# Four weight tiles of the first chunk fetched later, input transposes and score steps moved by some slots, three input tiles on another queue

## The chip, the cores and the metric

The kernel runs on one core of a Trainium2 chip. A core has five engines with an instruction stream each: TensorE (PE in the profile, with its weight loads shown apart as PEld), VectorE (DVE), ScalarE (ACT), GpSimd (POOL) and SyncE (SP). DMA transfers are issued from an engine's stream, here from SP and from ACT, and run beside the engines. The metric is the time of one execution on the device in microseconds (us). Three runs of the kernel before took 578.94, 583.47 and 583.84 us; their median is 583.47 us.

## What is computed

The input x has 2048 rows of 576 numbers in bfloat16. One layer norm feeds two branches, and the result is x plus both:

```python
xn = layernorm(x)                      # per row, no scale or shift
# A: sliding-window attention, 32 heads of 18, each query sees itself and the 255 keys before it
q, k, v = split(xn @ wqkv)             # 576 x 1728
o = softmax(mask(q @ k.T * 18**-0.5)) @ v
a = o @ wo                             # 576 x 576
# B: gated feed-forward layer
h = silu(xn @ w1) * (xn @ w3)          # 576 x 4608, twice
b = h @ w2                             # 4608 x 576
out = x + a + b
```

## The kernel before

**Chunks and phases.** The 2048 rows are worked off in four chunks (c = 0 to 3) of 512 rows, that is four tiles of 128 rows. Each chunk has two phases. The first runs 36 *units* (u = 0 to 35, loop at L824). A unit makes 128 of the 4608 hidden columns: nine *slots* (n = 0 to 8, L829), each a pair of matmuls (`unit_pairs`, L621), 18 matmuls in all. Then ScalarE takes a tanh (L629) and VectorE two multiplications (L635, L638) that leave the hidden columns in `hT`. The second phase multiplies `hT` with w2 (L671) and the attention's output with wo (L677), in two halves of 288 output columns, adds x and stores the result (L684, L686). Into the second phase are woven the projections of the next chunk (L399, L413).

**Attention between the units.** Into the slots of the first phase the loop puts *score steps* (`score_step`: four to six matmuls at L516, one exponential on ScalarE at L525, one or two mask multiplications on GpSimd at L552), 32 of them in chunk 0 and 40 in each later chunk. A step writes the two PSUM banks `SC`. When a quarter of the steps is done and 20 slots have gone by, a PV group follows (L573, 72 small matmuls); there are three in the first phase. Its result is scaled, transposed on VectorE and packed into `oT` by four or five small DMAs on SP's queue (`o_pack`, L606), over the next four units (`later`).

**The next chunk's input.** For each of the next chunk's four row tiles the loop places three things by tables of units (L785, L786): layer-norm statistics (`stat`), its application (`apply`), and the transpose `xn_turn` (`xt`: ten small transposes on PE at L370 into the same two banks `SC`, then one VectorE copy at L377 into `xnT`). In chunk 0 the four transposes stand in units 5, 9, 19 and 26.

**The planner.** A counter `clock` counts slots. `nxt` is the slot from which the next score step is due, and `soon` the earliest slot for it; after a transpose both are pushed on by `XT_AFTER` = 6 slots (L833), since the step overwrites the banks that the copy at L377 still reads. In chunk 0 the first step is due at slot 17 (L791). Nothing here is timed on the chip: the counter sets the order of the instructions, and the engines wait on each other by semaphores.

**Weights.** w3 and w1 come in fills of 512 hidden columns, so one fill serves four units. A fill (`load_w13`) is two halves of 576 KB: the w3 half is issued on SP's queue, the w1 half, from unit 3 on, on ACT's. Three buffers (`NW13` = 3) are used in turn. After unit 3, 7, 11, and so on to 31, the loop issues the fill that reuses the buffer just finished (L845, L846). In the text *fill f* is the one that units 4f to 4f+3 of chunk 0 read: fills 0, 1 and 2 are issued before the loop, fill 3 after unit 3, fill 6 after unit 15, fill 8 after unit 23. Fills issued after unit 27 and 31 are for the next chunk. w2 comes in tiles of 288 KB (`load_w2`, L327, always on SP's queue), four buffers in turn; 18 tiles serve a second phase. In chunk 0 the first four tiles are issued after units 8, 10, 12 and 14 (L881); every later one when the tile that it replaces has been used (L675).

**Queues.** SP issues, in the order of the program, the first weights, the fills' halves, `w2`, the x tiles, the small `repack` moves of q and k in the first units (L470), `o_pack` and the stores. A DMA issue takes its place in SP's stream, so one that has to wait holds up all behind it. ACT's queue carries the w1 halves, part of the `repack` moves and, at the start, two of the four x tiles.

```python
        for t in range(TB):
            xslot[t] = load_x(t, ("sp", "act")[t % 2])
...
                    if u in xt and n == 7:
                        xn_turn((c + 1) * TB + xt[u], SC)()
...
                if c == 0 and u in (8, 10, 12, 14):
                    load_w2()
```

Of the kernel before, what the change touches and what calls it, by code (L numbers as in the profile page):

```python
# [164 lines left out]
def bass_parallel_sum__sliding_block__glu_gated_swiglu__prompt_kernel(  # L165
# [32 lines left out]
    with ExitStack() as es:  # L198
# [93 lines left out]
        def load_x(t, eng="sp"):  # L292
            nonlocal xp_ctr
            s = xp_ctr % NXP
            xp_ctr += 1
            add(eng, lambda e: e.dma_start(xp[s][:], x2[t * 128:(t + 1) * 128, :]), w=[("xp", s)], dma=f"xp{s}")
            return s
# [391 lines left out]

        xslot = {}  # L690
        for t in range(TB):
            xslot[t] = load_x(t, ("sp", "act")[t % 2])
        add("sp", lambda e: e.dma_start(
            wa[:, 0:4, 2 * D:3 * D], A_wqkv[0:512, 2 * D:3 * D].rearrange("(kd p) f -> p kd f", p=128)),
            w=["wv"], dma="wv")
# [81 lines left out]
        aside = [m for g in held[3:] for m in repack_moves(0, g, "act")]  # L777
        aside_at = {u: 1 for u in (2, 3, 5, 6, 8, 9, 11, 14, 15, 17, 18, 21, 22, 24)}

        PV_COST, XT_COST, XT_AFTER, PV_AFTER = 6.6, 0.8, 6, 20  # L780

        for c in range(NC):
            NS = len(steps_of(c))
            att = [(g, s) for g in range(G) for s in range(NS)]
            near = {0: (2, 3, 5), 1: (6, 7, 9)} if c == 0 else {0: (0, 2, 4), 1: (4, 6, 8)}  # L785
            near.update({2: (15, 17, 19), 3: (23, 24, 26) if c == 0 else (24, 26, 28)})  # L786
            plan = near if c + 1 < NC else {}
            stat, apply, xt = ({v[k]: i for i, v in plan.items()} for k in range(3))
            loads = {0: () if c == 0 else (1,), 8: (2,), 17: (3,)} if c + 1 < NC else {}
            total = 9 * NF + len(att) + 3 * PV_COST + len(xt) * XT_COST  # L790
            start = 17 if c == 0 else 5  # L791
            last = total - 12
            nxt = soon = start
            clock = 0.0
            done = 0
            pv_ready = {}
            free = [("pt", n) for n in range(NPT)]
            if c:
                free += [("sh", n) for n in range(4)]
            early = [("h", n) for n in range(4)]  # L800
            side = {}
            jobs = {}
            next_pv = 0

            def later(u, what):
                side.setdefault(u, []).append(what)

            def take(n):
                if n < len(early) and c == 0:
                    return early[n]  # L810
                return free.pop(0)

            def score_step():
                nonlocal done
                g, s = att[done]
                scores(c, g, s)
                sl = take(done)
                exps(c, g, s, sl)
                masks(c, g, s)
                done += 1  # L820
                if done % (2 * NS) == 0:
                    pv_ready[done // (2 * NS) - 1] = clock + PV_AFTER

            for u in range(NF):  # L824
                if u in loads:
                    for i in loads[u]:
                        xslot[(c + 1) * TB + i] = load_x((c + 1) * TB + i)
                b0 = jobs[u] = job()
                for n in range(9):  # L829
                    if u in xt and n == 7:  # L830
                        xn_turn((c + 1) * TB + xt[u], SC)()
                        clock += XT_COST
                        nxt = soon = max(nxt, clock + XT_AFTER)  # L833
                    into = nxt - (clock + 9 - n)
                    if done < len(att) and (clock >= nxt or (n == 8 and into < 3 and clock >= soon)):
                        if not (u in xt and n < 7 and n > 1):
                            score_step()
                            soon = clock + 7.5
                            room = last - clock - PV_COST * (3 - next_pv) - 5 * sum(v > u for v in xt)
                            nxt = max(soon, clock + room / max(1, len(att) - done))  # L840
                            clock += 1
                    unit_pairs(c, u, n, n + 1, b0[0])
                    clock += 1
                unit_tanh(u, b0[0])
                if u % 4 == 3 and u < NF - 4:  # L845
                    load_w13((), "act")  # L846
                if next_pv in pv_ready and clock >= pv_ready[next_pv] and next_pv < 3:
                    j = next_pv
                    next_pv += 1
                    banks = job()  # L850
                    pv(c, j, banks)
                    clock += PV_COST
                    for g in (2 * j, 2 * j + 1):
                        for s in range(NS):
                            if pt_of[(c, g, s)][0] != "h":
                                free.append(pt_of[(c, g, s)])
                    later(u, lambda b=banks: (pv_out(b[0], 0), pv_out(b[1], 1), o_scale(0)))
                    later(u + 1, lambda j=j: (o_turn(2 * j, 0), o_turn(2 * j, 1), o_scale(1)))
                    later(u + 2, lambda j=j: (o_turn(2 * j + 1, 0), o_pack(2 * j, "sp")))
                    later(u + 3, lambda j=j: o_turn(2 * j + 1, 1))  # L860
                    later(u + 4, lambda j=j: o_pack(2 * j + 1, "sp"))
                unit_h(u, b0[0])
                for what in side.pop(u, []):
                    what()
                if u in stat:
                    t = (c + 1) * TB + stat[u]
                    for part in range(2):
                        ln_stats(t, xslot[t], part)
                if u in apply:
                    t = (c + 1) * TB + apply[u]  # L870
                    ln_apply(t, xslot[t])
                if c == 0 and u in (1, 6, 9):
                    repack(0, held.pop(0), "sp")
                if c == 0:
                    for _ in range(min(aside_at.get(u, 0), len(aside))):
                        aside.pop(0)()
                if c == 0 and u == 25:
                    add("sp", lambda e: e.dma_start(
                        wo[:, 0:4, :], A_wo[0:512, :].rearrange("(kd p) f -> p kd f", p=128)), w=["wo"], dma="wo")
                    add("sp", lambda e: e.dma_start(wo[0:64, 4, :], A_wo[512:576, :]), j=["wo"], dma="wo")  # L880
                if c == 0 and u in (8, 10, 12, 14):  # L881
                    load_w2()
                if u == 29:
                    xs = [load_x(c * TB + tt) for tt in range(TB)]
            assert done == len(att) and next_pv == 3 and not aside, (done, next_pv, len(aside))
            ring_of[:] = [*jobs[NF - 2], *jobs[NF - 1]]
            ring_ctr = 0
            ACC[:] = [*job(), *SC]
            proj = iter([])
            if c + 1 < NC:  # L890
                for g in range(G):
                    keep_keys(g)
                proj = (None for gen in (qk_atoms(c + 1, lambda c, g: repack(c, g, "act", ("act", "sp")[g % 2])), v_atoms(c + 1)) for _ in gen)
                xn_swap(c + 1, ("sp", "act"))
            proj_at = [36 + 8 * i for i in range(9)] + [116 + 24 * i for i in range(2 * TB)]
            banks = ()
            for n, item in enumerate(p2_list(c)):
                p2_item(c, item, xs)
                if n in (36, 70):
                    load_w13_half()  # L900
                if n == 3:
                    for u in sorted(side):
                        for what in side.pop(u):
                            what()
                elif n == 19:
                    banks = (ring(), ring())
                    pv(c, 3, banks)
                    pv_out(banks[0], 0)
                    pv_out(banks[1], 1)
                    o_scale(0)  # L910
                    o_turn(6, 0)
                    o_turn(6, 1)
                    o_pack(6, "act")
                    o_scale(1)
                    o_turn(7, 0)
                    o_turn(7, 1)
                    o_pack(7, "act")
                elif n == 100 and c + 2 < NC:
                    xslot[(c + 2) * TB] = load_x((c + 2) * TB)
                elif n in proj_at:  # L920
                    next(proj, None)
            for _ in proj:
                pass
# [31 lines left out]
```

## Time and profile before

| What | Value |
|---|---|
| median of three runs | 583.47 us (578.94, 583.47, 583.84) |
| the profiled execution: its own time | 584.11 us |
| its span, first to last instruction | 582.2 us |
| mean granted TensorE clock | 0.997 |
| PE busy | 567.8 us (98%) |
| DVE, ACT, POOL busy | 338.8 us (58%), 239.0 us (41%), 161.8 us (28%) |
| bytes by DMA | 83.60 MB, mean 144 GB/s |
| chunk 0: unit 0 starts, second phase starts | 24.48 us, 113.25 us |

The profile is taken by the hardware on one execution; its instruction times are exact to some ten nanoseconds, matmul ends are modelled. Busy shares are means over the whole span, and the stages have different limits: the start is set by loads, the first phase of each chunk by PE, and in chunk 0 by the DMAs beside it. Line numbers such as L621 are those of the kernel. `ps<-xnT,w` means that the PSUM tile `ps` is written from `xnT` and a tile whose name begins with `w`; buffer numbers are left out, so w13 and w2 buffers both appear as `w` and are told apart by line (L310 and L327) and size. The time of a DMA from issue to landing includes what it waits behind others in its queue.

### The profile page before, as it was taken

How to read it: one execution, taken by the hardware profiler on the slowest of the kernel's cores; microseconds unless marked ns; L12 is line 12 of the kernel's file. 1: busy time of each engine (PE TensorE's matmuls, PEld its weight loads, DVE VectorE, ACT ScalarE, POOL GpSimd, SP SyncE). 2: the span in 40 equal slices, each digit the busy share in tenths (PEclk: the TensorE clock that was granted, in tenths of full speed). 3: DMA queues.
4: the chain of work that ended last, by engine and by line, in shares of the span. 5: the costliest groups of instructions: out<-in, count | busy, mean ns of one | idle time of the engine just before them, and what ended most of it. 6: DMA issues, size and time to landing. Idle time of an engine off the chain costs nothing.

```text
span 582.2 us, 15317 instructions
## 1 busy us (share of the span) xinstructions
PE 567.8 (98%) x6548; PEld 337.9 (58%) x6558; DVE 338.8 (58%) x636; ACT 239.0 (41%) x310; POOL 161.8 (28%) x377
## 2 busy tenths in 40 slices
PE   8999979999999999999999999999999999999998
PEld 4445434567765555556776555446677554544776
DVE  7577956742348687764325868775331567667311
ACT  4166645400027677640003666862000577666000
POOL 6233433400004344540002343544000234433000
PEclk9999989999999999999999999999999999999999
DMA  8989998869644857776963567687676276541452
GB/s 227 189 151 183 168 195 181 168 135 197 163 118 85 171 105 140 158 149 143 196 149 95 127 133 156 119 165 163 137 169 150 74 143 124 136 91 52 122 154 62
DMA packets 118963, 83.60 MB, mean 144 GB/s; under 512 B 25520, under 2 KB 117808, under 8 KB 118896
## 3 DMA queue, kind: packets, MB, share of 16 engines
q1 hardware_dynamic: 82325, 60.31, 48.0%
q10 hardware_dynamic: 36571, 22.32, 20.0%
q8 instruction: 51, 0.84, 0.7%
q14 instruction: 16, 0.13, 0.1%
HBM read 71.07 MB, written 2.36 MB: 126 GB/s over the span
## 4 chain that ended last, share of the span: by engine, by line
PE 87%; DMA 5%; ACT 2%; DVE 2%; SPq 2%; issue 1%; ACTq 0%
PE ps L621 42%; PE ps L671 24%; PE ps L516 5%; PE ps L399 5%; PE ps L677 3%; PE ps L573 3%; DMA w<-in_B_w_dram 3%; PE ps L413 3%; DMA kv<-stage 1%; DMA wa<-in_A_wqkv_dram 1%; ACT pt L525 1%; SPq L470 1%; ACT th L629 1%; DVE hT L638 1%; DVE gs L635 1%
## 5 line engine op out<-in xcount | busy, mean ns | idle before, releaser
L525 ACT ACTIVATE pt<-ps 128x1024 bf16<-128x1024 f32 (+1 forms) x118 | 119.3, 1011 | 234.5 <-PE ps L516 233.0
L621 PE MATMUL ps<-xnT,w 64*128 64x512 bf16 x1440 | 190.6, 378 | 4.6 <-DMA w<-in_B_w_dram 4.5
L621 PE MATMUL ps<-xnS,w 64*128 64x512 bf16 x1152 | 156.3, 377 | 0.1
L671 PE MATMUL ps<-w,hT 128*128 128x288 bf16 x1152 | 154.8, 286 | 0.0
L552 POOL TENSOR_TENSOR pt<-pt,mk 128x128 int32<-128x128 int32 (+1 forms) x211 | 85.5, 428 | 237.2 <-ACT pt L525 236.8
L635 DVE SCALAR_TENSOR_TENSOR gs<-th,ps 128x512 bf16<-128x512 bf16 x144 | 98.1, 681 | 82.0 <-ACT th L629 81.2
L671 PEld LDWEIGHTS ps<-w,hT 128*128 128x128 bf16 x1152 | 112.0, 98 | 35.6 <-issue 1.7
L621 PEld LDWEIGHTS ps<-xnT,w 64*128 64x128 bf16 x1440 | 68.7, 94 | 66.3 <-DMA w<-in_B_w_dram 5.0
L638 DVE SCALAR_TENSOR_TENSOR hT<-gs,ps 128x512 bf16<-128x512 bf16 x144 | 98.9, 687 | 4.9
L629 ACT ACTIVATE th<-ps 128x512 bf16<-128x512 f32 x144 | 85.6, 594 | 38.4 <-PE ps L621 36.0
L621 PEld LDWEIGHTS ps<-xnS,w 64*128 64x128 bf16 x1152 | 57.4, 94 | 54.5 <-issue 1.5
L516 PE MATMUL ps<-qv,kv 64*128 64x320 bf16 (+2 forms) x720 | 58.5, 252 | 1.1 <-DMA kv<-stage 0.6
L516 PEld LDWEIGHTS ps<-qv,kv 64*128 64x128 bf16 x720 | 34.6, 94 | 38.8 <-issue 2.7
L684 DVE TENSOR_TENSOR ofin<-ps,xp 128x288 bf16<-128x288 f32 x32 | 14.7, 458 | 68.0 <-PE ps L677 68.0
L403 DVE CAST stage<-ps 128x512 bf16<-128x512 f32 x36 | 24.8, 689 | 36.0 <-PE ps L399 35.7
L428 DVE CAST va<-ps 64x288 bf16<-64x288 f32 x56 | 25.5, 455 | 28.8 <-PE ps L413 28.2
L399 PE MATMUL ps<-xnT,wa 128*128 128x512 bf16 x153 | 37.1, 379 | 0.4
L525 ACT ACTIVATE stage<-ps 128x1024 bf16<-128x1024 f32 x30 | 30.7, 1023 | 13.9 <-PE ps L516 13.7
L595 DVE STREAM_TRANSPOSE od<-oq 128x256 bf16<-128x256 bf16 x64 | 25.8, 427 | 6.3 <-POOL oq L588 6.3
L552 POOL TENSOR_TENSOR stage<-stage,mk 128x128 int32<-128x128 int32 (+1 forms) x54 | 21.9, 427 | 17.3 <-ACT stage L525 17.3
L588 POOL TENSOR_TENSOR oq<-uq,rden 128x288 bf16<-128x288 f32 x16 | 10.8, 674 | 53.1 <-DVE rden L587 53.1
L677 PE MATMUL ps<-wo,oT 128*128 128x288 bf16 x160 | 25.3, 286 | 0.0
(56 smaller groups left out, 271.5 us busy)
## 6 DMA issues: line engine op xcount, KB each, us to landing
w<-in_B_w_dram SPq DMA_DIRECT2D x42, 576.0 KB, 7.1
w<-in_B_w_dram SPq DMA_DIRECT2D x72, 288.0 KB, 3.4
w<-in_B_w_dram ACTq DMA_DIRECT2D x30, 576.0 KB, 8.3
xp<-in_A_x_dram SPq DMA_DIRECT2D x30, 144.0 KB, 5.9
out_dram<-ofin SPq DMA_DIRECT2D x32, 72.0 KB, 2.1
kv<-stage ACTq DMA_DIRECT2D x91, 18.0 KB
oT<-od SPq DMA_DIRECT2D x84, 18.0 KB
xnS<-xnT SPq DMA_DIRECT2D x5, 256.0 KB, 4.4
```

The lines of the kernel that those rows point to most:

```text
L399: add("pe", lambda e, kd=kd, ws=ws: e.matmul(PS[:, b, :], ws, xnT[:, c % 2, kd, :], start=(kd == 0), stop=(kd == 4)), r=["w8" if i == 8 el ...
L428: add("dve", lambda e, dst=dst, src=src: e.tensor_copy(dst, src), r=[("ps", b), ("ps", b + 1)], **kw)
L516: add("pe", lambda e, r0=r0, out_=out_, kb=kb, q0=q0, nb=nb: e.matmul(out_, kv[r0:r0 + 64, g, kb + NV - NB, :], qv[r0:r0 + 64, g, q0 * KB: ...
L525: add("act", lambda e: e.activation(pt_slot(sl)[:, 0:w, :], PS[:, SC[0]:SC[1] + 1, 0:w].rearrange("p r q -> p q r"), ACT.Exp, scale=scale) ...
L552: add("pool", lambda e, vb=vb, mm=mm: e.tensor_tensor(vb, vb, mm, ALU.mult), r=(key if n == 0 else []) + ["mk"], **{"w" if n == 0 else "j" ...
L595: add("dve", lambda e: e.transpose(od[i][:, c0:c0 + CH // 2], oq[:, c0:c0 + CH // 2]), r=["oq", "oq0"], **{"j" if half else "w": [("od", i)]})
L621: add("pe", lambda e, n=n, r0=r0, r=r, k=k, src=src: e.matmul(PS[:, b0 + r, :], w13[sl][r0:r0 + 64, k, fl * 128:(fl + 1) * 128], src, star ...
L629: add("act", lambda e: e.activation(th[i][:], PS[:, bg, :], ACT.Tanh, scale=0.5), r=[("ps", bg)], w=[("th", i)])
L635: add("dve", lambda e: e.scalar_tensor_tensor(out=gs[i][:], in0=th[i][:], scalar=1.0, in1=PS[:, bg, :], op0=ALU.add, op1=ALU.mult), r=[("t ...
L638: add("dve", lambda e: e.scalar_tensor_tensor(out=hT[:, u, :], in0=gs[i][:], scalar=0.5, in1=PS[:, bu, :], op0=ALU.mult, op1=ALU.mult), r= ...
L671: add("pe", lambda e: e.matmul(bank, hT[:, f, tt * 128:(tt + 1) * 128], w2[sl][:, k, :], start=(f == 0), stop=False), r=[("h", f), ("w2", ...
L677: add("pe", lambda e: e.matmul(bank, oT[:, k, tt * 128:(tt + 1) * 128], wo[:, k, d0:d0 + HD], start=False, stop=(k == 4)), r=[("oT", g) fo ...
```

## The change

It has four parts:

- In chunk 0 the first four w2 tiles are issued after units 20, 22, 24 and 26 rather than 8, 10, 12 and 14.
- The input transposes `xn_turn` stand before slot 8 of their unit rather than slot 7, in all chunks that have them. No score step is put into slots 2 to 8 of such a unit (before: 2 to 6).
- After a transpose the next score step is due 8 slots later in chunk 0 and 5 slots later in the other chunks (before: 6 in all). The first step of chunk 0 is due at slot 20 (before: 17).
- Of the first four x tiles, tile 0 is loaded by SP's queue and tiles 1, 2 and 3 by ACT's (before: 0 and 2 by SP's, 1 and 3 by ACT's).

```diff
         xslot = {}
         for t in range(TB):
-            xslot[t] = load_x(t, ("sp", "act")[t % 2])
+            xslot[t] = load_x(t, "act" if t else "sp")
...
-        PV_COST, XT_COST, XT_AFTER, PV_AFTER = 6.6, 0.8, 6, 20
+        PV_COST, XT_COST, PV_AFTER = 6.6, 0.8, 20
...
-            start = 17 if c == 0 else 5
+            start = 20 if c == 0 else 5
...
                 for n in range(9):
-                    if u in xt and n == 7:
+                    if u in xt and n == 8:
                         xn_turn((c + 1) * TB + xt[u], SC)()
                         clock += XT_COST
-                        nxt = soon = max(nxt, clock + XT_AFTER)
+                        nxt = soon = max(nxt, clock + (8 if c == 0 else 5))
                     into = nxt - (clock + 9 - n)
                     if done < len(att) and (clock >= nxt or (n == 8 and into < 3 and clock >= soon)):
-                        if not (u in xt and n < 7 and n > 1):
+                        if not (u in xt and n > 1):
                             score_step()
...
-                if c == 0 and u in (8, 10, 12, 14):
+                if c == 0 and u in (20, 22, 24, 26):
                     load_w2()
```

## The prediction

> **What bounds the kernel.** First the busy times and the slices of the page.
>
> ```profile
> PE 567.8 (98%) x6548; PEld 337.9 (58%) x6558; DVE 338.8 (58%) x636; ACT 239.0 (41%) x310; POOL 161.8 (28%) x377
> ...
> DMA  8989998869644857776963567687676276541452
> ```
>
> PE is busy for all but 14.4 of 582.2 us. The change removes no matmul, so nearly all that it can win is PE's idle time. The DMA row shows where loads could matter: its first six slices (14.55 us each, up to 87 us) read 8 or 9. So next, PE's waits:
>
> ```profile
> PE ps L621 <- DMA w<-in_B_w_dram: 4.5, 2, 4.1
> ...
> PE ps L370 <- ACT pt L525: 1.1, 5, 0.3
> ...
> PE ps L516 <- DMA kv<-stage: 0.6, 1, 0.6
> PE ps L413 <- DMA wa<-in_A_wqkv_dram: 0.6, 1, 0.6
> PE ps L516 <- DVE xnT L377: 0.5, 2, 0.2
> ```
>
> Each is a wait that one part of the change touches. The largest is for a fill. PE's timeline puts both in chunk 0: 0.39 us at 71.89 (unit 20, fill 5) and 4.12 us at 84.78 (unit 24, fill 6). The chain that ended last, around the second:
>
> ```profile
> 65.39 1.62 PE ps L621 x15
> 67.01 17.72 DMA w<-in_B_w_dram
> 84.73 0.05 issue
> 84.78 3.25 PE ps L621 x12
> ```
>
> Fill 6's w3 half was issued at 67.01 and landed 17.72 us later. SP's timeline shows what it stood behind:
>
> ```profile
> 57.83 0.48 SPq L327 DMA_DIRECT2D w<-in_B_w_dram  x1
> 58.36 0.93 SPq L310 DMA_DIRECT2D w<-in_B_w_dram  x1
> 59.33 3.31 SPq L327 DMA_DIRECT2D w<-in_B_w_dram  x1
> 62.69 3.77 SPq L606 DMA_DIRECT2D oT<-od  x4
> 66.49 0.47 SPq L327 DMA_DIRECT2D w<-in_B_w_dram  x1
> 67.01 0.70 SPq L310 DMA_DIRECT2D w<-in_B_w_dram  x1
> ```
>
> L327 are w2 tiles, not read before 113.25; L310 are the w3 halves of fills 5 and 6. ACT's half of fill 6 went out at 61.38, when unit 15 had freed the buffer: SP was 5.6 us later. The stages (columns: busy us of the five engine rows, then granted clock, DMA share, GB/s):
>
> ```profile
> 84.78:88.03 3.25, 3.25 (x20) 1.23 (x22) 1.03 (x3) 0.00 (x0) 0.38 (x2) 0.57 1.15 201
> ...
> 25.00:85.00 60.00, 54.52 (x706) 27.36 (x704) 44.06 (x83) 34.16 (x46) 20.45 (x49) 0.99 1.05 170
> 92.00:108.00 16.00, 15.76 (x236) 7.84 (x236) 12.56 (x23) 9.95 (x14) 5.63 (x13) 1.00 0.66 145
> ```
>
> From 25 to 85 us the DMAs are saturated at 170 GB/s, from 92 to 108 a third is free. After the long wait the clock was 0.57.
>
> **The w2 tiles.** Nothing is added or dropped: four issues of 0.4 to 3.3 us on SP and 4 x 288 KB = 1.18 MB move by some 25 us. At 170 GB/s the bytes are 6.9 us of DMA time, 1.73 a tile. Does every fill then come in time? I take each landing of before, less the tiles no longer ahead of it, against the new start of its unit.
> - Fill 5: landed 71.85 (58.36 + 13.5), two tiles fewer: 68.4. Unit 20 could have started at 71.50. Earlier waits that go (below: 0.3 + 0.5 + 0.24) bring it to 70.46; the second PV group (69.78 to 71.11, 1.33) and two steps of 0.2 now follow unit 20's start, so 68.7. A dead heat: 0.3 of slack. I keep 0.1 us of its 0.39.
> - Fill 6: landed 84.73, four tiles fewer: 77.8. Unit 24: 84.78 - 4.12 - 0.39 - 1.04 - one step 0.2 = 79.0. Slack 1.2. The 4.12 us go.
> - Fill 7: ACT's half landed at 83.8 (69.90 + 13.9), SP's between the x tile before it (73.44 + 12.9 = 86.4) and fill 8, by bytes near 90.7; less 6.9: 83.8. Unit 28: units 24 to 27 took 11.63 (84.78 to 96.41); without the slow clock's 1.31 (below), a wait of 0.24, a PV group (1.0) and one step it is 8.9, so 87.9. Slack 4.
> - Fill 8: landed 95.74 (81.47 + 14.3), less 6.9, plus the two tiles now ahead of it, 3.5: 92.3. Unit 32: units 28 to 31 took 8.6 (to 105.0), with the PV group and a step more 9.8, so 97.7. Slack 5.4.
>
> What is late next is thus fill 5, then fill 6, by about a microsecond. On SP the tiles are moved past `o_pack`; fill 6's half now stands ahead of the first `o_pack`, which is a unit later with its PV group, so it can go at 61.4. The last w2 tile goes out after unit 26, near 86; even with the longest landing seen, 17.7, it is there at 103.7, before the second phase (113.25 less the 7.0 us that chunk 0 saves in all: 106.2).
>
> The clock: at 84.78 18 matmuls took 3.25 us; the same 18 take 1.94 elsewhere. So 1.31 us more go with the wait, 5.43 in all. After the 0.39 us wait the matmuls kept their 1.03 to 1.04 us for eight.
>
> The Trainium skill, "TensorE: Matmul & The Clock Gate" (Part 1: The HAM clock gate), says that the clock falls to half after an idle window of about 3.4 us and stays so for a window; by it the loss would be an estimated 1.7 us and the sum 0.4 higher, and a remainder under 3.4 us might cost no clock. The trace agrees in kind, with 1.31.
>
> **First steps of chunk 0.** The first step waited 0.60 us at 28.93 for the small `repack` moves, which landed at 28.88. Three slots later (3 x 1.94 / 9 = 0.65) PE passes 28.93 with other matmuls; as PE itself comes earlier, I take 0.5 (bounds 0 and 0.6). The same 32 steps are issued; each delays its exponential (0.9 to 1.0 us, ACT 41% busy) and masks (0.43 each, POOL 28%) equally.
>
> **Transposes.** In chunk 0 the step after a transpose waited 0.24 us twice for the copy at L377; it stands two to three slots (0.43 to 0.65) later: 0.48 gone. VectorE's copy comes at most one slot later. In chunks 1 and 2 the transposes waited for the exponential of the step before, which reads the same banks: 1.1 us in five waits (0.15 to 0.26). One more pair of matmuls ahead of each covers 0.216: I take 1.0 (at most 1.1). The next step stays where it was, five pairs behind rather than six. In chunk 1 the first copy ended at 180.90 and the step began at 181.49; it would begin at 181.27, still after the copy. If that cover of 0.37 is gone, six steps wait some tenths and the term turns to about -1, its lower bound.
>
> **x tiles.** SP loses one issue of 0.42 us ahead of the projection weights, for which PE waited 0.58 at 8.91; ACT gets one more ahead of a 1.28 us table load that ends at 3.0, its first real work coming at 6.89. Bounds: nothing, as the last weights took 6.7 us to land and the bytes are the same, and 0.43. Nearest row: the issue. I take 0.3.
>
> The Trainium skill, "DMA: Bandwidth & Descriptors" (Issuing engines are not separate DMA queues), says that DMAs of several engines share the same DMA engines, and that spreading saves issue time only. By that, with the bytes unchanged, this term might be 0 and the sum 0.3 lower; no run here shows it yet.
>
> **Sum.** 5.43 + (0.39 - 0.1) + 0.5 + 0.48 + 1.0 + 0.3 = 8.0 us; at most 8.4. The profiled execution took 584.11 us (span 582.2 and 1.9 around it), 0.64 above the median. 584.11 - 8.0 = **576.1 us**.
>
> **Rivals.**
> - *The wait comes back in part* at unit 20 or 24. For: both slacks are near one microsecond, an estimate from a mean rate; one run of before was 5 us faster, so landings vary. Against: fills 5 and 6 lose exactly the bytes that stood ahead. A wait of 2 to 5 us: 578 to 581.
> - *It doesn't do what it says*: the small moves, not the w2 tiles, hold fill 6 up, and the 5.43 stay. For: 128-byte pieces ride in the same queues. Against: two w2 tiles landed 13.8 and 16.8 us after issue, within the same stretch. Only the other terms, 2.6: 581.5.
> - *Slower: the second phase starves.* The tiles' 6.9 us of DMA time meet 5.4 free us between 92 and 108 (a third of 16), in a first phase 7.0 shorter: a backlog of up to 8.5 us where the second phase starts. Its fifth tile is asked for when the first is used up and took 5.5 us (issue at 115.42). Four tiles of 16 matmuls last 7.9 us; from there on a longer fetch stops PE. 5.5 + 8.5 is 6 too long; with the clock (1.3) and as much again on the next tiles, 9: 585. Against: a PV group and the projections lie between, and L671 has no DMA wait now.
>
> **Chances.** Forecast (574.5 to 578) 0.64, returning wait 0.20, no effect 0.09, starving 0.07. One per cent, about what a measurement can tell from no change, is 5.8 us, so the bounds are 577.6 and 589.3: most of the first case lies below 577.6 (0.56); its rest (0.08), the next two (0.29) and a mild starving (0.03) lie within; starving through many tiles lies above 589.3 (0.04). The range is the first two cases, 574.5 to 581.
>
> **What would show it.** Right: no PE wait over 0.5 us between 25 and 113, fill 6's SP half issued near 61.4 and landed before 79, the second phase starting near 106, no dip of the clock, no wait of L370 on L525. Wrong: a fill's wait at units 20 to 32; a DMA wait at L671 soon after the second phase starts; new waits of L516 on L377 in chunks 1 and 2.

## The result and the profile after

The changed kernel takes **576.09 us** (median of 8 runs, 574.94 to 577.53) and the kernel before 582.84 us (median of 8, 578.94 to 584.25): a ratio of 0.9898, 95% interval 0.9867 to 0.9928. It is faster by 1.0%. The forecast was 576.1. A second series gave 574.88 (6 runs) against 583.15, ratio 0.9864, interval 0.9833 to 0.9895.

The profiled execution took 574.94 us, 1.1 less than the median, with a span of 573.1 us; that of before took 584.11, 1.3 more than its median. So the two profiles stand 9.2 us apart, and the medians 6.7. This matters below.

The page, parts 1 and 2, and then PE's waits of the whole span, all of them:

```profile
PE 565.3 (99%) x6548; PEld 337.8 (59%) x6558; DVE 338.6 (59%) x636; ACT 238.5 (42%) x310; POOL 161.4 (28%) x377
...
DMA  8989999998627585877762658696666367441552
```

```profile
PE ps L702 <- DVE oq L697: 1.2, 1, 1.2
PE ps L573 <- issue: 1.0, 2, 0.7
PE ps L357 <- DVE xn L347: 0.9, 2, 0.7
PE ps L621 <- DMA w<-in_B_w_dram: 0.5, 1, 0.5
PE ps L413 <- DVE va L428: 0.3, 1, 0.3
```

All five waits that the prediction listed are gone. L370 on L525, L516 on the small moves and L516 on L377 are not in the list any more; at L413 a wait of 0.3 us for VectorE stands where 0.58 for the weights stood; the one wait for a fill that is left, 0.45 us, is a new one (fill 3, at unit 12). The chain that ended last runs on PE up to unit 24's start (78.55) and passes there to ScalarE, where before it ran 17.72 us through a DMA:

```profile
76.33 1.94 PE ps L621 x18
78.27 0.24 PE ps L516 x4
78.51 0.02 issue
78.53 0.02 ACT pt L525
```

SP's timeline for the same stretch. L310 "x2" holds the halves of fills 5 and 6 (56.24 and 60.3), L606 are the first `o_pack` moves, the L310 at 69.61 belongs to fill 7, L327 is the first w2 tile:

```profile
56.24 4.73 SPq L310 DMA_DIRECT2D w<-in_B_w_dram  x2
61.51 3.15 SPq L606 DMA_DIRECT2D oT<-od  x4
...
69.61 0.83 SPq L310 DMA_DIRECT2D w<-in_B_w_dram  x1
70.48 0.63 SPq L327 DMA_DIRECT2D w<-in_B_w_dram  x1
```

And two of the stages shown of before (busy us of PE, PEld, DVE, ACT, POOL; clock, DMA share, GB/s):

```profile
92.00:108.00 16.00, 16.00 (x225) 8.94 (x202) 12.51 (x22) 9.25 (x14) 8.82 (x22) 1.00 1.13 208
25.00:85.00 60.00, 59.34 (x766) 28.95 (x764) 47.19 (x90) 35.73 (x49) 21.52 (x52) 1.00 0.95 169
```

PE is idle for 0.66 of 60 us in the first phase of chunk 0, where it was 5.48. The DMAs have lost their slack between 92 and 108 us: two of the moved w2 tiles land in it (at 93.91 and 101.79), and with chunk 0 shorter the fills of the next chunk come earlier too.

### The profile page after: what moved, and what is told of

Read it like the earlier page. It is cut to its first block, busy times and chain, and to the rows that moved or that the text cites. A ratio compares the mean times of both kernels' runs of the same rounds, so it can differ in the third digit from the quotient of the medians.

```text
span 573.1 us, 15316 instructions
## 1 busy us (share of the span) xinstructions
PE 565.3 (99%) x6548; PEld 337.8 (59%) x6558; DVE 338.6 (59%) x636; ACT 238.5 (42%) x310; POOL 161.4 (28%) x377
## 4 chain that ended last, share of the span: by engine, by line
PE 91%; DMA 3%; DVE 3%; SPq 1%; issue 1%; ACTq 0%; POOL 0%; ACT 0%
PE ps L621 45%; PE ps L671 24%; PE ps L399 6%; PE ps L516 6%; PE ps L573 4%; PE ps L677 3%; PE ps L413 3%; DMA w<-in_B_w_dram 3%; SPq L470 1%; DVE xn L347 1%; DMA xp<-in_A_x_dram 0%; DVE va L428 0%; PE ps L370 0%; DVE hT L638 0%; DVE gs L635 0%
## 5 line engine op out<-in xcount | busy, mean ns | idle before, releaser
L525 ACT ACTIVATE pt<-ps 128x1024 bf16<-128x1024 f32 (+1 forms) x118 | 119.3, 1011 | 228.5 <-PE ps L516 227.0
L671 PE MATMUL ps<-w,hT 128*128 128x288 bf16 x1152 | 154.8, 286 | 0.1
L671 PEld LDWEIGHTS ps<-w,hT 128*128 128x128 bf16 x1152 | 112.0, 98 | 35.7 <-issue 1.9
L516 PE MATMUL ps<-qv,kv 64*128 64x320 bf16 (+2 forms) x720 | 58.5, 252 | 0.2
L516 PEld LDWEIGHTS ps<-qv,kv 64*128 64x128 bf16 x720 | 34.8, 94 | 37.2 <-ACT stage L525 1.5
L525 ACT ACTIVATE stage<-ps 128x1024 bf16<-128x1024 f32 x30 | 30.7, 1023 | 13.7 <-PE ps L516 13.5
```

The lines of the kernel that those rows point to most:

```text
L516: add("pe", lambda e, r0=r0, out_=out_, kb=kb, q0=q0, nb=nb: e.matmul(out_, kv[r0:r0 + 64, g, kb + NV - NB, :], qv[r0:r0 + 64, g, q0 * KB: ...
L525: add("act", lambda e: e.activation(pt_slot(sl)[:, 0:w, :], PS[:, SC[0]:SC[1] + 1, 0:w].rearrange("p r q -> p q r"), ACT.Exp, scale=scale) ...
L671: add("pe", lambda e: e.matmul(bank, hT[:, f, tt * 128:(tt + 1) * 128], w2[sl][:, k, :], start=(f == 0), stop=False), r=[("h", f), ("w2", ...
```

## The experiments

Fill landings are the time of issue plus the time to landing of the later half. In each table row, "before" is the kernel before in the same series.

| Kernel | Median us | before | Ratio, 95% interval | Executions with clock 0.999 or 1.000 |
|---|---|---|---|---|
| w2 tiles moved, nothing else (`w2_only`) | 578.18 | 582.13 | 0.9942 (0.9915 to 0.9969) | 10 of 10 |
| third and fourth tile moved (`w2_two`) | 577.61 | 582.13 | 0.9913 (0.9881 to 0.9945) | 9 of 10 |
| tiles at the old units, by ACT's queue (`w2_by_act`) | 581.80 | 582.13 | 0.9990 (0.9960 to 1.0019) | 3 of 10 |
| changed kernel, tiles moved back (`undo_w2`) | 578.71 | 582.13 | 0.9949 (0.9922 to 0.9976) | 9 of 10 |
| slots alone (`slots_only`, 4 runs) | 577.12 | 583.25 | 0.9898 (0.9838 to 0.9958) | 4 of 4 |
| slots alone again (`slots_again`) | 577.41 | 583.15 | 0.9907 (0.9874 to 0.9939) | 6 of 6 |
| changed kernel again (`after_again`) | 574.88 | 583.15 | 0.9864 (0.9833 to 0.9895) | 6 of 6 |
| x tiles alone (`x_only`) | 583.58 | 583.25 | 1.0020 (0.9985 to 1.0055) | 2 of 10 |
| matmuls into the wait (`keep_busy`) | 583.21 | 583.25 | 0.9999 (0.9962 to 1.0036) | 7 of 10 |
| first `o_pack` later (`opack_later`) | 583.49 | 583.15 | 1.0007 (0.9972 to 1.0042) | 5 of 10 |
| tiles later still (`w2_late`, 4 runs) | 576.05 | 583.15 | 0.9892 (0.9847 to 0.9937) | 4 of 4 |

A second profile of the unchanged kernel (`before_again`) took 585.78 us.

The last column counts the executions in which the mean granted clock of TensorE shows no dip. It speaks for executions that were not profiled: the profiled one of before has 0.997 with one dip, `before_again` 0.994 with one twice as long. Of the 67 executions of before in these series 26 had 0.999 or 1.000 (median 579.9 us), 29 had 0.997 (583.3 us) and 12 had 0.994 to 0.996 (586.3 us).

### The w2 tiles alone

```diff
-                if c == 0 and u in (8, 10, 12, 14):
+                if c == 0 and u in (20, 22, 24, 26):
```

> The kernel before with one edit: the first four w2 tiles are issued after units 20, 22, 24 and 26. Theory (their bytes hold up fills 5 and 6): fill 5 lands near 68.4 and fill 6 near 77.8 us, ahead of units 20 (70.9) and 24 (80.3); the waits of 0.39 and 4.12 us and the slow clock's 1.31 go, 5.8 us in all: 578.3 for an execution like the profiled one of before (584.11), ratio about 0.990. Rival (the slots and the x tiles carry the gain, the w2 tiles little): the wait of 3 to 4 us at unit 24 stays, within 1 us of before.

Its profiled execution took 578.22 us, 5.89 less than the one of before: the 5.8 forecast for it. Fill 5 was there at 66.4 (56.4 + 10.0), fill 6 at 73.3 (63.2 + 10.1); units 20 and 24 began at 70.97 and 79.57. PE's waits in this kernel between 25 and 113 us:

```profile
PE ps L516 <- DMA qv<-stage: 0.7, 1, 0.7
PE ps L516 <- DVE xnT L377: 0.6, 3, 0.2
```

No fill among them. The rival falls: the tiles alone remove both waits, and the clock was full in all ten executions. But the median fell by 3.95 only, since the median execution of before (582.13) is 2.0 faster than the profiled one.

### Two tiles moved

```diff
+                if c == 0 and u in (8, 10, 20, 22):
```

> The kernel before with only the third and fourth w2 tiles moved, to after units 20 and 22; the first two stay after units 8 and 10. Theory (1.73 us of DMA time a tile): fill 5 lands as before (wait of 0.4 at unit 20), fill 6 lands 3.5 us earlier, near 81.2: a wait of 0.6 at unit 24, and no dip of the clock. About 4.8 us faster than before in an execution like the profiled one, 579.3. Rival (the four issues on SP, not the bytes): fill 6's half leaves near 62 to 63 us and the wait goes wholly.

Two tiles are enough: units 20 and 24 began at 71.47 and 80.07 with no wait (unit 12 waited 0.71 us for fill 3), and the time is that of moving all four within the intervals. The 1.73 us a tile would have left 0.6 us, so the price per tile was too low. Fill 6's half left at 65.0, not at 62 to 63.

### The tiles on ACT's queue

```diff
-            add("sp", lambda e: e.dma_start(
+            add(eng, lambda e: e.dma_start(          # eng = "act" for the first four tiles
                 w2[s][:], ...
```

> The kernel before, but the four w2 tiles go out at the same units 8, 10, 12 and 14 on ACT's queue rather than SP's. Same bytes at the same time; SP's stream is free of their issues, so fill 6's half can go 3 to 5 us earlier. Theory (bytes): fill 6 is whole near 84 us all the same, now with ACT's half the late one; a wait of 3 to 5 us in all at units 20 and 24 stays, 582 to 585 us. Rival (late issue on SP, or the order in SP's queue, is what makes fill 6 late): the wait goes, about 578.

No difference in the median, as the theory had it; but not in its way. In the profiled execution (581.41) fill 6's SP half left at 65.45 and landed 15.1 us later, at 80.6, and unit 24 began at 82.57 without a wait. The time had been lost ahead of it: unit 0 began at 25.40 rather than 24.48, which the edit cannot have done, as the first moved tile goes out at 46.77; units 12 and 20 waited 0.66 and 0.26 us. But this execution had the full clock, and seven of the ten had 0.997, the figure of the profiled before: in most of them a dip remained, as the theory would have it, though no profile shows where. Which of the two theories is right this run does not tell.

### The changed kernel with the tiles moved back

> The changed kernel with the w2 tiles back after units 8, 10, 12 and 14. Theory: fills 5 and 6 land as in before, 71.9 and 84.7; units 20 and 24 come earlier than in before (68.6 and 78.6), so PE waits some 3 us at unit 20 and 2 to 3 at unit 24, 5 to 6 us in all; each is shorter than the 4.12 of before, so the clock may stay full. 581 to 583 us, about 5.5 above the changed kernel. Rival (the gain is in the other parts): 577.

Between the two: taking the tiles back costs 2.6 us against the changed kernel's 576.09, half of what was expected. PE's waits from 25 us to the second phase:

```profile
PE ps L573 <- issue: 1.8, 1, 1.8
PE ps L621 <- DMA w<-in_B_w_dram: 1.1, 2, 0.8
PE ps L621 <- issue: 0.2, 1, 0.2
```

The fills cost 1.1 us, at units 12 and 20, not 5 to 6. (The stall of 1.8 us in the PV group, of which the last section tells, comes ahead of unit 24, which began at 81.86; without it fill 6 would have been some 0.8 us late there.) Fill 6's SP half left at 63.4 and landed 17.4 us later, at 80.9, with all four w2 tiles ahead of it; I had it at 84.7.

### The slots alone

Only the placing of transposes and score steps is changed; w2 and x tiles as before.

> The kernel before with the slots alone: transposes and score steps placed as in the changed kernel; w2 tiles and x tiles as in before. Two theories after the first four runs. One (order in SP's queue): the first PV group comes a unit later, so the first o_pack stands behind fill 6's half, which leaves near 63.5 rather than 67.0 and lands near 81; unit 24 starts near 82 with under 1 us of wait and no slow clock. 3 us below before, 579.5. The other (only the bytes of the w2 tiles count): fill 6 lands near 84.7, units 20 and 24 wait 5 us in all; no more than the 2.0 us of the other waits is won, 580.5 to 582.

577.12 us, ratio 0.9898: as much as the whole change in its first series. The second theory is wrong, and the first expected too little. In the profiled execution (574.60) fill 6's half left at 61.35 and landed 15.4 us later, at 76.8; unit 24 began at 78.57:

```profile
57.50 0.48 SPq L327 DMA_DIRECT2D w<-in_B_w_dram  x1
58.03 1.72 SPq L310 DMA_DIRECT2D w<-in_B_w_dram  x1
59.80 1.51 SPq L327 DMA_DIRECT2D w<-in_B_w_dram  x2
61.35 0.65 SPq L310 DMA_DIRECT2D w<-in_B_w_dram  x1
62.05 5.07 SPq L606 DMA_DIRECT2D oT<-od  x4
```

Against SP's lines of before, the first `o_pack` (L606) now stands behind fill 6's half instead of ahead of it, because the first PV group comes a unit later.

### That order alone

```diff
-                    later(u + 2, lambda j=j: (o_turn(2 * j + 1, 0), o_pack(2 * j, "sp")))
+                    late = 1 if c == 0 and j == 0 else 0
+                    later(u + 2, lambda j=j: o_turn(2 * j + 1, 0))
+                    later(u + 2 + late, lambda j=j: o_pack(2 * j, "sp"))
```

> The kernel before with one edit in SP's stream alone: the first o_pack (four small DMAs that wait for VectorE) is issued a unit later, behind fill 6's half instead of ahead of it. PE, DVE, ACT and POOL keep their order; the w2 tiles stay after units 8, 10, 12, 14. Theory (the order in SP's stream makes fill 6 late): its half leaves near 61.5 rather than 67.0 and lands near 77 to 79, the wait at unit 24 goes, 3 to 5 us below before, near 578.5. Rival (the four tiles' bytes ahead of it): it lands at 83 to 85 all the same, no difference. Second rival (the later score steps and PV group, not the order in the queue, made the two slots kernels fast): no difference either.

No difference. SP's order is now that of the slots kernel, and yet fill 6's half left at 64.6 and landed 19.1 us later, at 83.7: the issues of the two w2 tiles before it held SP for 4.23 us, where they took 1.51 in the slots kernel. PE's waits up to 115 us, in part:

```profile
PE ps L621 <- DMA w<-in_B_w_dram: 3.0, 2, 2.2
...
PE ps L621 <- DVE hT L638: 0.8, 1, 0.8
PE ps L370 <- DVE xn L347: 0.6, 1, 0.6
```

The wait at unit 24 is halved, and 1.4 us of new waits for VectorE take its place, where before had none. So the theory that the order in SP's stream is enough falls. What also differs between this kernel and the slots kernels is how fast the DMAs went from 58 to 78 us. The windows of before, of a second execution of before, of this kernel, and of the two profiles of the slots alone, in that order:

```profile
58.00:78.00 20.00, 19.47 (x272) 9.61 (x270) 16.65 (x34) 12.02 (x17) 8.52 (x22) 1.00 1.17 167
```

```profile
58.00:78.00 20.00, 20.00 (x280) 9.90 (x276) 16.74 (x34) 12.61 (x18) 8.79 (x22) 1.00 1.17 171
```

```profile
58.00:78.00 20.00, 18.96 (x268) 9.41 (x264) 15.72 (x31) 11.93 (x18) 8.65 (x21) 1.00 1.16 165
```

```profile
58.00:78.00 20.00, 20.00 (x280) 9.95 (x278) 17.07 (x36) 13.16 (x18) 8.84 (x21) 1.00 1.12 195
```

```profile
58.00:78.00 20.00, 19.29 (x272) 9.37 (x270) 16.21 (x33) 11.98 (x17) 8.44 (x20) 1.00 1.11 190
```

165 to 171 GB/s in these three without the slots, 190 and 195 with them, the DMAs saturated in both (share over 1.1). In 20 us that is 0.4 to 0.6 MB more, at about 180 GB/s two to three microseconds. Within before, the rate falls where many small packets pass: from 62 to 66 us 140 GB/s with 358 of 993 packets under 512 B, from 54 to 58 us 208 GB/s with 41 of 1057. But in the slots kernel the four microseconds from 58 have 683 of 1701 packets under 512 B and 197 GB/s. And the slots are not needed for the higher rate. Without them, the tiles on ACT's queue (`w2_by_act`) show it as well, and two tiles moved (`w2_two`) 186 GB/s:

```profile
58.00:78.00 20.00, 19.09 (x270) 9.41 (x268) 15.33 (x31) 11.79 (x16) 8.88 (x21) 1.00 1.16 191
```

`undo_w2`, with the slots, has 183; `x_only` and `keep_busy`, which keep the slots and the tiles of before, 173 and 172. So the low rate goes with the slots of before and all four tiles on SP's queue together. Which of the moved things makes the DMAs faster is not settled; that small packets meet w2 tiles and fills at other moments is only a guess.

### Slots alone and the changed kernel, side by side

> The slots alone once more, beside the changed kernel on the same chip. If the order in SP's stream is enough, the w2 tiles add nothing to it: within 1 us of the changed kernel, both near 576 to 577. If the tiles count for themselves (taking them back cost 2.6 us in an earlier run): 578 to 579 here, 576 there.

> The changed kernel beside the slots alone. 576 us, ratio near 0.990; fill 6 there by 72, 6 us ahead of unit 24; a wait of about half a microsecond for fill 3 at unit 12.

577.41 and 574.88 us: the tiles and the x tiles together add 2.5 us to the slots, the intervals of the ratios just overlapping (0.9874 to 0.9939 and 0.9833 to 0.9895). Taking the tiles alone back (`undo_w2`) cost 2.6, between two series. So the tiles most likely count for themselves, by some 2.5 us on top of the slots; without the slots it is 3.4 to 4 us (0.58% of 582, and 3.95). In the changed kernel fill 6 was whole at 70.4 in this execution (61.0 + 9.4, ACT's half), 9 us ahead of unit 24; in `slots_again` at 79.7, 1.0 ahead. The wait for fill 3 at unit 12 was 0.98 us rather than half a microsecond.

### The x tiles alone

> The kernel before with the x tiles' queues alone. Expected: the projections' last small weight piece is issued 0.47 us earlier on SP, PE's wait of 0.58 us at 8.91 goes, unit 0 starts near 24.0 rather than 24.5; the waits for fills 5 and 6 stay. 0.3 us (0 to 0.5) below before, within the spread of its runs. Rival (the earlier landing of the first weights seen in the changed kernel, 7.3 rather than 8.9, is how that one execution went): unit 0 near 24.5.

The time shows nothing, as expected; the profile shows the part. Unit 0 began at 23.91. In all five profiles of kernels with this edit it began between 23.88 and 23.94, and the last small piece of the v weights landed between 6.9 and 7.3 us. In the nine profiles without it unit 0 began between 23.96 and 25.40, and that piece landed at 7.2 to 7.6 in three and at 8.3 to 8.9 in six. So the edit gives up to 0.5 us, and above all gives it every time. The rival (chance) is half right: without the edit, too, some executions have the early landing. One part of the expectation failed: fills 5 and 6 landed at 71.1 and 83.1, still late, but no wait for them was seen, because PE had lost 3.43 us in the second PV group just before unit 20 (74.36; unit 24 began at 85.40). The last section says more on that stall.

### Matmuls into the wait

```diff
                 b0 = jobs[u] = job()
+                if c == 0 and u == 24:
+                    for k in range(18):
+                        add("pe", lambda e: e.matmul(PS[:, b0[0], :], ident[:], xnT[:, 0, 0, :], start=True, stop=True), ...)
```

The 18 results are overwritten by unit 24.

> The kernel before with 18 matmuls more (128x512, results overwritten) ahead of unit 24 of chunk 0, 3.9 us at full clock. Theory (the slow 18 matmuls after the wait are the clock, which drops because PE stood idle): where the wait at unit 24 would be 4 us, PE works through it, the clock stays 1.00 and unit 24 takes 1.94 us: 1.3 us below before in such an execution; where the wait is shorter, the added matmuls cost the difference, up to 3.9 us more than before. Rival (they are slow because weights land at the same time): the unit takes 3.2 us all the same.

The stage of units 24 to 27, in this kernel and in before:

```profile
84.35:94.63 10.28, 10.04 (x173) 4.96 (x175) 6.66 (x13) 5.03 (x7) 2.69 (x7) 1.00 0.96 187
```

```profile
84.78:96.41 11.63, 11.39 (x172) 5.23 (x174) 6.66 (x13) 5.03 (x7) 2.73 (x7) 0.88 0.90 179
```

The same work took 1.35 us less, at a clock of 1.00 rather than 0.88, while the DMAs moved more, not less. The rival (weights landing) falls; the slow matmuls are the clock, and the clock fell because PE stood idle, as far as one profile shows it. The median is unchanged, presumably because the added 3.9 us cost what they save where the wait is shorter. In three of the ten executions the clock was 0.997; no profile shows where it dipped in these.

### Before once more

> The kernel before once more, for a second profile. If the wait at unit 24 makes its spread of 578 to 586 us, then the wait in this execution and its time differ from the first profile's (4.12 us, 584.11) by the same amount, with the slow clock (1.3 us) there only if the wait is long.

It does not bear the expectation out. The wait at unit 24 was 4.02 us, 0.1 shorter than in the first profile, and the time 1.7 longer. The clock made the larger part of the difference:

```profile
84.59:97.23 12.64, 12.37 (x172) 5.65 (x174) 6.49 (x13) 5.03 (x7) 2.73 (x7) 0.81 0.86 170
```

12.64 us for the stage that takes 10.28: 2.4 us lost to the clock, where the first profile lost 1.35. The clock was half for 6.83 us here, from 82.60 on, and for 3.41 us there, from 84.15 on. Unit 12 waited 0.48 for fill 3 besides. So the spread of before is not the length of one wait. The 67 executions sort by the clock instead: medians of 579.9, 583.3 and 586.3 us for no dip, 0.997 and less. Each step is more than the clock alone costs (1.35 and 2.4 us in the two profiles), as the long wait goes with the dip.

### The tiles later still

```diff
+                if c == 0 and u in (28, 30, 32, 34):
```

> The changed kernel with the four w2 tiles after units 28, 30, 32 and 34. The DMAs are less busy up to 85 us and have 1.18 MB more to move from there to the second phase. Theory: in the changed kernel the second phase's fifth tile landed 0.4 us before its use; here the queue is 3 to 6 us longer at that point, so L671 waits 2 to 5 us for the fourth or fifth tile: 578 to 581. Rival (the DMAs catch up): no wait over 0.5 us at L671, 576.

No wait in the second phase, 576.05 us; the rival is right. The third tile, issued at 102.2, and the fourth, at 107.0, landed ahead of their use, and the fifth took 8.9 us from its issue at 109.06, less than the 11.0 of the changed kernel. The DMAs catch up.

## Why the prediction was right, and where its working was not

**The number.** 576.1 was forecast and 576.09 measured. Some of that is luck: the sum was made against an execution 1.3 us above its kernel's median and took 8.0 off; the profiles differ by 9.2 and the medians by 6.7 (8.3 in the second series). The split was not right: by medians the tiles alone brought 3.4 to 4 us, where 5.72 was forecast, and the slots alone 5.4 to 6, where 2.0 was. The two gains overlap, as both edits remove the same wait; that the sum of the terms came out all the same is luck.

**The signs** that the prediction set for being right all came in the first profile. In the second (`after_again`) the wait at unit 12 was 0.98 us, over its limit of 0.5, and L671 waited 0.80 us once, 27 us into the second phase; L671 waits of 0.5 to 1.1 us occur in profiles with the tiles at their old units as well (1.11 in `before_again`).

**The wait for fills 5 and 6, 5.72 us with the clock.** Its size was right for the profiled execution: moving only the tiles brought 5.89. The order of the work carried too: units 20, 24, 28 and 32 were forecast to begin at 68.7, 79.0, 87.9 and 97.7, the second phase at 106.2; they began at 68.64, 78.55, 87.31, 97.20 and 105.73.

**The step that failed** is the one that takes "each landing of before, less the tiles no longer ahead of it". It made the tiles' bytes the cause of the wait and 170 GB/s a constant. Fills 5, 6 and 7 were forecast for 68.4, 77.8 and 83.8 and were whole at 64.6 (56.2 + 8.4), 70.6 (60.3 + 10.3) and 77.8 (69.6 + 8.2): what I called a dead heat had 4 us to spare. Fill 8 came at 92.0, forecast 92.3. And with all four tiles still ahead of it, fill 6 landed at 76.8 and 79.7 in the two profiles of the slots alone, where the step says 84.7; with the tiles alone moved it was whole at 73.3, where the step says 77.8. The waits were on an edge, and either of two edits was enough to clear it.

**First steps and transposes.** With it the slots as a whole were mis-sized: 0.5 + 0.48 + 1.0 = 2.0 us, where the slots alone gave 5.4 to 6 (0.93% and 1.02% of 583). The terms themselves came as listed: the steps' and the transposes' waits are gone from the list. The transposes wait for L525 in all eight profiles without the slots and in none of the six with them; the first step still waited 0.28 us in `after_again`. From the second phase of chunk 0 to the end, where only the transposes count, 468.95 us became 467.40: 1.55, forecast 1.0 (466.1 to 468.4 in the six profiles, 468.3 to 469.9 in the eight). What was left out is that the same edit moves the PV groups, and so fill 6's half in SP's stream, from 67.0 to 61.4, and that the DMAs run faster beside it (why is open). I had the first as a side remark and gave it no price.

**x tiles.** 0.3 of at most 0.43 forecast; unit 0 came 0.54 earlier. The Trainium skill, "DMA: Bandwidth & Descriptors" (Issuing engines are not separate DMA queues), lets a second issuer save issue time only. The piece was issued 0.47 us earlier (1.71 rather than 2.18) and landed 1.6 earlier (7.26 rather than 8.87); part of this is the scatter that kernels without the edit show as well, so the runs neither contradict the rule nor show that issue time is all.

**The rivals.** The wait did not come back at units 20 or 24, but 0.45 us of it did at unit 12, for fill 3, which the working never looked at: fill 3's SP half left at 41.6, behind the `repack` moves and the ACT half of fill 4 (41.3), and landed at 50.2, while unit 12 had become 1 us earlier. In the six profiles of kernels with the slots this wait was 0.45 to 1.3 us, and 0.5 to 0.7 in three of the eight without them. The starving second phase had its backlog: the fifth tile took 11.0 us rather than 5.5 (14 was the bound). It cost nothing, with 0.4 us to spare: the tile was issued at 107.89, landed at 118.87 and was needed at 119.29, 11.4 us after its issue. The limit I set, four tiles of matmuls or 7.9 us, counted one tile too many, as only three lie between, and left out the PV group and the projections; the rival named them and did not count them.

**Clock.** The dip is gone with the wait. The Trainium skill, "TensorE: Matmul & The Clock Gate" (Part 1: The HAM clock gate), would have had an estimated 1.7 us for one window at half clock. The runs show 1.35 and 2.4 in two executions of before, the second with a dip twice as long. With the idle window of about 3.4 us they agree only in part: idle times of 1.8 us (`undo_w2`) and 2.2 us (`opack_later`) left the clock full, but it fell 2.0 us after PE went idle in `before_again` and 2.2 us after in `x_only`, and 3.5 us after in before.

## What to carry to other kernels

A wait for a load in a saturated stretch can have more than one cause. Before crediting it to the bytes ahead, list everything that shifts when the load is issued, on each queue, and ask what each would do alone; here two edits that share no line each removed the same 4 us, and their gains did not add up. Sum against the profile, but know where that execution stands among the others: a wait at the edge, and the dip of the clock that goes with a long one, make the kernel's spread, and the median gains less than a profile taken on the long side.

## What the runs showed of the hardware

- Saturated DMAs are not at one rate. With the share over 1.1 in all, the 20 us from 58 to 78 ran at 165 to 173 GB/s in the five profiles that keep the slots of before and all four tiles on SP's queue, and at 183 to 195 in five others, where the slots, the tiles' queue or two of the tiles were moved. Why is open.
- PE can stall for nothing that the profile's waits name. In `x_only` it stood 3.43 us, in `undo_w2` 1.78, in the same place of chunk 0, with the DMAs saturated; in `x_only` the clock fell for it (0.59 from 74.0 to 80.5 us), which ate what that edit gained:

```profile
73.72 0.29 PE L573 MATMUL ps<-pt,va 64*20 64x128 bf16 x4 [3.43 <-issue]
```

The traces point at late instructions. The page lists 51 instruction packets of 16 KB (its queue q8) for the 13,106 instructions of PE and PEld in before, one for each 257. In `x_only` the stall began at 70.29, such a packet ran from 70.37 to 71.88, and PE went on at 73.72, 1.84 us after its end; in `undo_w2` the packet ended at 73.27 and PE went on at 74.83. Of the stalls of 0.2 us and more that the fourteen profiles put down to nothing ("issue"), all 40 end 1.2 to 1.9 us after the end of such a packet, and all lie at the same place within every 256 instructions of PE's stream, to about a dozen. No run changed the packets, so this is read from the times and not tested.

- The dips of the clock had one length or twice that. The clock was half for 3.41 us in the first profile of before, and for 6.83 in the second and in `x_only`. When it fell PE stayed idle for another 0.6 us in the first case, and for 2.0 and 1.2 us in the other two.
